# A long convolution and a mode mix by matmul transforms: 45 classes of 128 become 90 classes of 64, with other tiles, buffers and dependency tokens

## The chip, the core and the metric

The kernel runs on one core of one Trainium2 chip. The metric is the time of one execution on the device in microseconds (us); the profile is one execution taken by the hardware profiler. Engines are named as in the profile: PE (matrix engine; PEld is its weight loads), DVE (vector), ACT (scalar), POOL (GpSimd), SP (the engine that issues most DMAs).

## What is computed

```python
B, S, D, n_modes = 8, 5696, 128, 64
def conv(x, h):                       # x [B,S,D], h [S,D]
    L = 2 * S
    Y = rfft(x, n=L, axis=1) * rfft(h, n=L, axis=0)[None]
    return irfft(Y, n=L, axis=1)[:, :S]
def mix(x, w_r, w_i, w_ch):           # w_r, w_i [64,D,D], w_ch [D,D]
    X = rfft(x, axis=1); Y = zeros_like(X)
    Y[:, :64] = complex product of X[:, :64] with w_r + i w_i, per mode
    u = x + irfft(Y, n=S, axis=1)
    return u + maximum(u @ w_ch, 0)
out = mix(conv(x, h), ...)            # float32 [8,5696,128]
```

## The kernel before, in words

The sequence of 5696 is padded to N = 45 x 128. Every transform is a set of matmuls with constant matrices in 16-bit floats, in three steps: over the 45 blocks (constant `F`), then, in each of 45 classes, over the 128 positions in a block (six matrices `M`, real and imaginary parts, each 128 x 5760), then the product with the transformed filter `Hs`, and the way back.

Sequences are taken in pairs (`g_` = 0 to 3). The order of the work is the order in which the Python code adds it, engine by engine:

- **Start.** h is loaded by POOL, the first three `M` by SP, then x of pair 0 by POOL. 16 tiles transform h (128 matmuls of 45 rows), 12 tiles make `Hs`, then 32 tiles `a_tile` (line 338) transform x of pair 0: 8 matmuls of 45 rows each, four per sequence, the two sequences on partitions 0 to 44 and 64 to 108. The evacuation `evac` (line 246) alternates between ACT and DVE. `xtile` gives two PSUM slots of two banks in turn.
- **Ticks.** `tick` (line 365) runs 27 times per pair, two classes a tick. It loads two classes of `Gs` by SP, makes 8 matmuls with `M` (256 columns), ACT copies the result to `Xs`, and DVE makes the complex product by two multiplications (`Pb`, `Xs`) and two half-size additions (`y_part`, line 421). Three ticks later 8 matmuls transform back (`ps<-Xs,M`), ACT or, in one class of eight, DVE copies to `Zs`, and SP writes it to the DRAM scratch `zscr`. Four ticks later 4 matmuls with `Gs` accumulate the 64 low modes in bank 7. Four `Zs` buffers exist. The last four ticks also carry 16 a tiles of the next pair; 16 more follow, and then POOL loads the x after that (`next_x`, line 350). Behind pair 2 it loads the mode weights `W` in eight DMAs instead.
- **Join.** When pair 3 is done, SP loads `IBs`, the `ZT` buffers are cleared in part, 256 matmuls of 8 columns mix the modes, 16 transposes turn them, giving `C`.
- **Output.** `load_zt` (line 496) reads 16 positions of `zscr` back, 45 rows twice, rows 128 KB apart. `u_tile` (line 505) adds the modes' part (360 columns) and the last step over the classes (16 matmuls of 45 columns), 64 tiles in all. `o_tile` (line 525) multiplies four blocks by `[w_ch, I]`, ACT makes `R` (relu), DVE adds (`O`), SP writes 256 KB out. 96 such tiles run, three per two u tiles, and 24 are left at the end. u tiles have two PSUM slots, o tiles two others.

Waits are not written by hand. `Recorder.add` (line 55) derives them from tokens: an operation waits for the last writer of each token that it reads, and for the last writer and all readers of each token that it writes. Tokens need not match memory. In `o_tile` both evacuations write the tokens `HST` of the old filter, whose place their buffers take:

```python
R.add("scalar", lambda e: e.activation(rv, src_r, RELU), bk, [("r", i % NR)] + HST)
R.add("vector", lambda e: e.tensor_tensor(ov, src_u, rv, ADD), bk + [("r", i % NR)], [("o", i % NO)] + HST)
```

Of the kernel before, what the change touches and what calls it, by code (L numbers as in the profile page):

```python
# [4 lines left out]
P = 128  # L5
F16 = mybir.dt.float16
# [117 lines left out]
def bass_long_conv_fft__then__afno_spectral_mix_kernel(nc, x, h, moe_w_r, moe_w_i, moe_w_ch, out):  # L124
# [63 lines left out]
    KW = NQ * P  # L188
    a_m = take(6 * KW * 2)
    m_sb = [at(f"M{i}", KW, F16, a_m + i * KW * 2) for i in range(6)]  # L190
    h_in = at("Hin", P * D, F16, a_m + 3 * KW * 2)
    a_h = take(2 * KW * 2)
    h_sb = at("Hs", 2 * KW, F16, a_h)
    SLOT = 2 * D
    a_as = take(NQ * 2 * SLOT * 2)
    a_sb = at("As", NQ * 2 * SLOT, F16, a_as)
    a_x = take(P * D * 2)
    x_sb = at("Xin", P * D, F16, a_x)
    NG, NX, NB_, NZ = 5, 5, 3, 4
    a_g = take(NG * 1024)  # L200
    g_sb = [at(f"Gs{i}", 512, F16, a_g + i * 1024) for i in range(NG)]
    a_xs = take(NX * 2048)
    x_s = [at(f"Xs{i}", 1024, F16, a_xs + i * 2048) for i in range(NX)]
    a_pb = take(NB_ * 2048)
    p_b = [at(f"Pb{i}", 1024, F16, a_pb + i * 2048) for i in range(NB_)]
    a_zz = take(NZ * 2048)
    z_s = [at(f"Zs{i}", 1024, F16, a_zz + i * 2048) for i in range(NZ)]
    xm = at("XM", B * P, F16, take(2048))
    xt = at("XT", B * P, F16, take(2048))
    xtn = at("XTn", B * 64, F16, take(1024))  # L210
    f1_sb = at("F1", 2 * NQ, F16, take(2 * NQ * 2))
    fq_sb = at("FQ", NQ, F16, take(NQ * 2))
    wi_sb = at("WI", 2 * P, F16, take(512))

    NC = 4
    zt = [at(f"ZT{i}", 4096, F16, a_as + i * 8192) for i in range(NC)]
    ib_sb = at("IBs", KW, F16, a_as + NC * 8192)
    u_sb = [at(f"UT{i}", KW, F16, a_m + i * KW * 2) for i in range(4)]
    NR, NO = 3, 6
    r_sb = [at(f"R{i}", 512, F32, a_h + i * 2048) for i in range(NR)]  # L220
    o_sb = [at(f"O{i}", 512, F32, a_h + (NR + i) * 2048) for i in range(NO)]
    w_sb = at("W", 2 * M * D, F16, a_x)
    yr = at("YR", 512, F16, a_pb)
    yi = at("YI", 512, F16, a_pb + 1024)
    c_sb = at("C", B * P, F16, a_xs)
# [12 lines left out]
    for name, n in (("c", 16), ("x", 12), ("g", 8), ("z", 8), ("w", 16), ("t", 10), ("o", 10)):  # L238
        R.ring(name, n)
# [26 lines left out]


    dma("sync", f1_sb[:, :], c_f1.ap(), "c", (), [("f1",)])
    dma("sync", h_in[NQ - 1:NQ, 64 * D:], c_z.ap(), "c", (), [("hz",)])
    for p0 in (0, 64):  # L270
        dma("sync", x_sb[p0 + NQ - 1:p0 + NQ, 64 * D:], c_z.ap(), "c", (), [("xz", p0)])

    def load_rows(dst, src, off, p0, tok):
        half = 64 * D
        for c in range(2):
            dma("gpsimd", dst[p0:p0 + NQ - 1, c * half:(c + 1) * half],
                bass.AP(src.tensor, src.offset + off + c * half, [[P * D, NQ - 1], [1, half]]),
                "x", (), [tok + (c,)])
# [324 lines left out]
```

## Time and profile before

| what | us |
|---|---|
| three runs | 628.93, 630.63, 630.70 |
| median | 630.63 |
| span of the profiled execution | 636.9 |
| PE busy / PEld busy | 470.4 / 380.9 |
| DVE / ACT / POOL busy | 351.5 / 326.6 / 27.3 |
| share of the last-ending chain: DMA, PE, DVE, ACT | 33%, 28%, 17%, 16% |

The profiled execution's own time is its span, 636.9 us, 6.3 us above the median of the runs. Busy time is an average over the span; the stages differ, so the stretches below are read one by one. [...]

### The profile page before, as it was taken

How to read it: one execution, taken by the hardware profiler on the slowest of the kernel's cores; microseconds unless marked ns; L12 is line 12 of the kernel's file. 1: busy time of each engine (PE TensorE's matmuls, PEld its weight loads, DVE VectorE, ACT ScalarE, POOL GpSimd, SP SyncE). 2: the span in 40 equal slices, each digit the busy share in tenths (PEclk: the TensorE clock that was granted, in tenths of full speed). 3: DMA queues.
4: the chain of work that ended last, by engine and by line, in shares of the span. 5: the costliest groups of instructions: out<-in, count | busy, mean ns of one | idle time of the engine just before them, and what ended most of it. 6: DMA issues, size and time to landing. Idle time of an engine off the chain costs nothing.

```text
span 636.9 us, 11755 instructions
## 1 busy us (share of the span) xinstructions
PE 470.4 (74%) x4924; PEld 380.9 (60%) x4924; DVE 351.5 (55%) x592; ACT 326.6 (51%) x479; POOL 27.3 (4%) x42
## 2 busy tenths in 40 slices
PE   0647769598879598878698868994565877787665
PEld 0647667487667487667487657882543656565432
DVE  0223558398449388448388458883221555555544
ACT  0213547377646476447476547873021555555543
POOL 3000010000010000010000001111200000000000
PEclk9999658799659699559799559998575999999955
DMA  8996119856219856209856209999979999999544
GB/s 155 212 206 252 48 14 144 191 149 179 68 22 139 199 159 169 59 14 148 197 159 169 59 2 147 239 238 244 176 130 181 277 345 346 332 306 341 214 167 167
DMA packets 97546, 110.86 MB, mean 174 GB/s; under 512 B 23147, under 2 KB 81659, under 8 KB 92923
## 3 DMA queue, kind: packets, MB, share of 16 engines
q1 hardware_dynamic: 79398, 92.77, 50.8%
q0 software_dynamic: 18096, 17.35, 19.7%
q8 instruction: 38, 0.62, 0.4%
q14 instruction: 14, 0.11, 0.1%
HBM read 80.53 MB, written 46.92 MB: 200 GB/s over the span
## 4 chain that ended last, share of the span: by engine, by line
DMA 33%; PE 28%; DVE 17%; ACT 16%; issue 5%; SPq 0%; DVEq 0%; ACTq 0%
PE ps L265 28%; DMA zscr<-Zs 8%; DMA M<-cM 7%; DVE O L543 7%; ACT R L542 6%; DMA W<-in_moe_w_i_dram 6%; ACT As L255 5%; DMA W<-in_moe_w_r_dram 5%; DMA out_dram<-O 4%; DMA ZT<-zscr 4%; DVE As L259 4%; ACT Xs L255 2%; DVE Xs L427 2%; DVE Pb L387 2%; DVE Zs L257 1%
## 5 line engine op out<-in xcount | busy, mean ns | idle before, releaser
L265 PE MATMUL ps<-As,M 128*128 128x256 f16 (+1 forms) x900 | 116.2, 283 | 15.8 <-DMA M<-cM 9.5
L259 DVE TENSOR_SCALAR As<-ps 128x720 f16<-128x720 f32 x72 | 67.8, 942 | 94.5 <-PE ps L265 94.5
L265 PE MATMUL ps<-Xs,M 128*128 128x256 f16 x720 | 100.3, 284 | 23.5 <-ACT Zs L253 20.1
L255 ACT ACTIVATE Xs<-ps 128x1024 f16<-128x1024 f32 (+1 forms) x92 | 92.5, 1007 | 46.5 <-PE ps L265 46.2
L255 ACT ACTIVATE As<-ps 128x720 f16<-128x720 f32 x72 | 61.0, 847 | 92.7 <-PE ps L265 92.7
L265 PEld LDWEIGHTS ps<-As,M 128*128 128x128 f16 x900 | 87.8, 107 | 31.6 <-DMA M<-cM 9.7
L253 ACT CAST Zs<-ps 128x512 f16<-128x512 f32 x160 | 88.2, 596 | 35.1 <-DMA zscr<-Zs 26.6
L265 PE MATMUL ps<-F,Xin 45*128 45x90 f16 x1024 | 81.8, 331 | 27.6 <-ACT As L255 15.7
L543 DVE TENSOR_TENSOR O<-ps,R 128x512 f32<-128x512 f32 x96 | 63.1, 658 | 63.5 <-PE ps L265 30.7
L265 PE MATMUL ps<-WI,UT 128*128 128x256 f16 x360 | 70.2, 325 | 35.1 <-DVE O L543 31.5
L265 PEld LDWEIGHTS ps<-F,Xin 45*128 45x128 f16 x1024 | 72.2, 269 | 39.6 <-ACT As L255 21.3
L265 PEld LDWEIGHTS ps<-Xs,M 128*128 128x128 f16 x720 | 71.2, 101 | 37.8 <-ACT Zs L253 20.9
L387 DVE TENSOR_TENSOR Pb<-Xs,Hs 128x1024 f16<-128x1024 f16 (+1 forms) x92 | 62.3, 677 | 56.8 <-ACT Xs L255 56.4
L542 ACT ACTIVATE R<-ps 128x512 f32<-128x512 f32 x96 | 54.9, 572 | 65.4 <-DVE O L543 61.3
L427 DVE TENSOR_TENSOR Xs<-Xs,Pb 128x512 f16<-128x512 f16 (+1 forms) x184 | 77.5, 421 | 0.1
L265 PEld LDWEIGHTS ps<-WI,UT 128*128 128x128 f16 x360 | 42.2, 156 | 56.5 <-DVE O L543 54.6
L265 PE MATMUL ps<-Zs,Gs 128*128 128x256 f16 x360 | 62.7, 290 | 11.5 <-DVE Zs L257 9.8
L391 DVE TENSOR_TENSOR Xs<-Xs,Hs 128x1024 f16<-128x1024 f16 (+1 forms) x92 | 62.0, 674 | 0.1
L265 PEld LDWEIGHTS ps<-FQ,ZT 109*128 109x128 f16 x1024 | 44.3, 101 | 23.3 <-DMA ZT<-zscr 11.2
L265 PE MATMUL ps<-FQ,ZT 109*128 109x45 f16 x1024 | 49.5, 189 | 9.5 <-DMA ZT<-zscr 9.5
L265 PEld LDWEIGHTS ps<-Zs,Gs 128*128 128x128 f16 x360 | 35.3, 104 | 23.3 <-DVE Zs L257 15.3
L265 PE MATMUL ps<-IBs,C 128*128 128x360 f16 x128 | 44.2, 345 | 3.9 <-issue 3.2
(38 smaller groups left out, 199.2 us busy)
## 6 DMA issues: line engine op xcount, KB each, us to landing
ZT<-zscr SPq DMA_DIRECT2D x64, 360.0 KB, 7.5
zscr<-Zs SPq DMA_DIRECT2D x88, 256.0 KB, 3.2
out_dram<-O SPq DMA_DIRECT2D x88, 256.0 KB, 6.1
Xin<-in_x_dram POOLq DMA_DIRECT2D x16, 704.0 KB, 18.3
Gs<-cG SPq DMA_DIRECT2D x88, 128.0 KB, 3.4
M<-cM SPq DMA_DIRECT2D x6, 1440.0 KB, 18.2
W<-in_moe_w_r_dram POOLq DMA_DIRECT2D x4, 512.0 KB, 7.3
W<-in_moe_w_i_dram POOLq DMA_DIRECT2D x4, 512.0 KB, 8.7
```

What stands on the lines that cost most here:

```text
L253: R.add(e, lambda h_: h_.copy(dst, src), reads, writes)
L255: R.add(e, lambda h_: h_.activation(dst, src, COPY, scale=scale), reads, writes)
L257: R.add(e, lambda h_: h_.tensor_copy(dst, src), reads, writes)
L259: R.add(e, lambda h_: h_.tensor_scalar_mul(dst, src, scale), reads, writes)
L265: R.add("tensor", lambda h_: h_.matmul(o, l, r, start=st, stop=sp), reads, writes)
L387: R.add("vector", lambda e: e.tensor_tensor(pbv, xv, hv[1], MULT), [tx] + HST, [tp])
L391: R.add("vector", lambda e: e.tensor_tensor(xv, xv, hv[0], MULT), [tx], [tx])
L427: R.add("vector", lambda e: e.tensor_tensor(a, a, b, ADD if part else SUB), [("xs", s % NX), ("pb", s % NB_)], [("xs", s % NX), ("y", s % ...
L542: R.add("scalar", lambda e: e.activation(rv, src_r, RELU), bk, [("r", i % NR)] + HST)
L543: R.add("vector", lambda e: e.tensor_tensor(ov, src_u, rv, ADD), bk + [("r", i % NR)], [("o", i % NO)] + HST)
```

## The change

The transform length becomes 2S = 11392 = 178 x 64, so that a real transform has 90 classes of 64 positions (89 blocks go in). In parts:

- **First transform:** an a tile has four matmuls of 89 rows, both sequences in one 128-wide weight, 180 columns. Three or four PSUM slots are used outside the ticks, two in the last three ticks, which carry 12 a tiles; 20 follow.
- **Filter:** H's first transform puts real and imaginary part into the two halves of the partitions (weights of 64 columns). The second makes `[hr; hi]` by a matmul of 128 columns of weights, and `[hi; hr]` by two of 64, in each of 90 classes. It now stands behind pair 0's a tiles and behind the issue of pair 1's x.
- **Second transform:** four classes a tick, 16 matmuls of 64 rows and 128 columns, the two sequences in the two halves of the rows. `M` is one 64-row strip, stored twice (4.4 MB instead of 8.8).
- **Product:** two multiplications, `U1` and `U2`, read from ACT's copy in two ticks of three and from PSUM in the third. The additions are left to the third transform, whose two weights `W1`, `W2` are constant: 4 matmuls of 512 columns a tick. ACT makes both copies to `Zs`.
- **Modes:** `G` is loaded once, after H has left its place. Modes lag by three ticks, the third transform by two; a pair has 26 ticks. The turning of the modes moves behind the last pair.
- **Output:** `ZT` has 90 rows, both parts in one DMA of 16 positions, five buffers, no clearing; the twiddles move into the last step's constant `S4` (2.05 MB, loaded behind `IBs`). A u tile covers 8 positions: 16 matmuls of 89 columns and two of 356. u and o tiles share a ring of four PSUM slots; `O` has 12 buffers. `once` puts a token of a reused place only on the first writer.

The core of the diff, cut:

```diff
--- before.py
+++ after.py
@@ -125,50 +125,55 @@
...
+    J = 64
+    NQ = S // J
...
+    KT = 4
+    NT = (NK + KT - 1) // KT
...
+    NU, NXS, NZ = 3, 2, 4
...
+    ZB = 16
+    NC = 5
...
+    next_x(0)
...
+    for i in range(MP):
+        lo, hi = i * KP * 3 * J, (i + 1) * KP * 3 * J + (J if i == MP - 1 else 0)
+        dma("sync", m_sb[:, lo:hi], bass.AP(c_m, lo, [[MW, P], [1, hi - lo]]), "c",
+            HT[:2] if i < 2 else XIN[:2] if i < 4 else [], [("m", i)])
...
+    XSLOT = [0, 2]
+    ZBANK = [4, 5, 6]
     MB = 7
...
     for j in range(16):
-        t = xtile()
+        t = turns("s", [0, 2, 4, 6])
...
+            for ri in range(2):
+                mm(pv(t + i // 4, (i % 4) * NK, [[1, NK]], J * ri, J),
+                   ap(h_in, J * D, 0, NQ, d, [[D, J]]), ap(f1_sb, 2 * NK, 0, NQ, ri, [[2, NK]]),
+                   True, True, HT, [bank(t + i // 4)])
...
+    def a_tile(j, slots):
+        t = turns("s", slots)
+        for i in range(4):
+            d = 4 * j + i
+            mm(pv(t + i // 2, (i % 2) * 2 * NK, [[1, 2 * NK]]),
+               ap(x_sb, 2 * J * D, 0, NQ, d, [[D, 2 * J]]), f1_sb[0:NQ, :], True, True,
+               XIN + [("f1",)], [bank(t + i // 2)])
...
+    for j in range(32):
+        a_tile(j, [0, 2, 4, 6])
+    next_x(1)
...
+    for t in range(NT):
+        n = len(ticks[t])
+        sl = turns("s", [0, 2, 4, 6])
+        for i, k in enumerate(ticks[t]):
+            col = k * 3 * J + J
+            rd = AHT + mtok(k) + [("g", k // KP)]
+            for o, w, c_, p0 in ((0, P, col, 0), (P, J, col + J, 0), (P, J, col, J)):
+                mm(pv(sl + i // 2, (i % 2) * 256 + o, [[1, P]], p0, w), m_sb[:, c_:c_ + w],
+                   ah_sb[:, k * D:(k + 1) * D], True, True, rd, [bank(sl + i // 2)])
+        evac(bass.AP(h_sb, KT * t * D, [[2 * HW, P], [D, n], [HW, 2], [1, D]]),
+             pv(sl, 0, [[256, n], [P, 2], [1, D]]),
+             [bank(sl), bank(sl + 1)], [("h", t)])
+    for i in range(MP):
+        lo, hi = i * KP * P, (i + 1) * KP * P
+        dma("sync", g_sb[:, lo:hi], bass.AP(c_g, lo, [[GW, P], [1, hi - lo]]), "c", (), [("g", i)])
...
+    LC, LM = 2, 3
...
+        i = t % NU
+        hv = [bass.AP(h_sb, r * HW + KT * t * D, [[2 * HW, P], [0, 2], [1, n * D]]) for r in range(2)]
+        uv = [bass.AP(u, 0, [[1024, P], [512, 2], [1, n * D]]) for u in (u1[i], u2[i])]
+        if t % 3 != 2:
+            e = (t - t // 3) % NXS
+            xv = bass.AP(x_s[e], 0, [[1024, P], [512, 2], [1, n * D]])
+            evac(xv, src, bk, [("xs", e)], eng="scalar")
+            src, bk = xv, [("xs", e)]
+        for r in range(2):
+            R.add("vector", lambda e, r=r: e.tensor_tensor(uv[r], src, hv[r], MULT),
+                  bk + [("h", t)], [("u", i, r)])
...
+            for i, k in enumerate(ticks[t]):
+                for r in range(2):
+                    for b in range(2):
+                        col = k * 3 * J + (J if r == 0 else 0) + b * J
+                        mm(pv(sl + b, i * D, [[1, D]]),
+                           ap(m_sb, MW, J * b, J, col, [[1, P]]),
+                           ap(a_sb, AW, J * b, J, (2 * k + r) * D, [[1, D]]), r == 0, r == 1,
+                           AST + mtok(k), [bank(sl + b)])
+            products(t, t)
...
+            s_ = t - LC
+            n = len(ticks[s_])
+            i, zi = s_ % NU, s_ % NZ
+            zb = [turns("z", ZBANK) for b in range(2)]
+            for b in range(2):
+                for r in range(2):
+                    mm(pv(zb[b], 0, [[1, n * D]]), (W1, W2)[r], (u1, u2)[r][i][:, b * 512:b * 512 + n * D],
+                       r == 0, r == 1, [("u", i, r), ("wc",)], [bank(zb[b])])
+                evac(bass.AP(z_s[zi], b * D, [[1024, P], [2 * D, n], [1, D]]),
+                     pv(zb[b], 0, [[D, n], [1, D]]), [bank(zb[b])], [("zs", zi, b)], eng="scalar")
+            zo = (g_ * NK + KT * s_) * P * 256
+            dma("sync", bass.AP(zs, zo, [[256, P], [P * 256, n], [1, 256]]),
+                bass.AP(z_s[zi], 0, [[1024, P], [256, n], [1, 256]]), "z",
+                [("zs", zi, 0), ("zs", zi, 1)], [("zd", g_, s_)])
...
+            s_ = t - LM
+            zi = s_ % NZ
+            for i, k in enumerate(ticks[s_]):
+                mm(pv(MB, 0, [[1, 256]]), g_sb[:, k * P:(k + 1) * P], z_s[zi][:, i * 256:(i + 1) * 256],
+                   k == 0, k == NK - 1, [("g", k // KP), ("zs", zi, 0), ("zs", zi, 1)], [bank(MB)])
...
+            for j in range(12, 32):
+                a_tile(j, [0, 2, 4])
+            if g_ + 2 < NP:
+                next_x(g_ + 2)
+            else:
+                load_w()
...
+    def once(key, toks):
+        if key in first:
+            return []
+        first[key] = 1
+        return list(toks)
+
+    dma("sync", ib_sb[:, :], c_ib.ap(), "c", (), [("ib",)] + once("ib", M_ALL))
+    dma("sync", s4_sb[0:NK, :], c_s4.ap(), "c", (), [("s4",)] + once("s4", M_ALL))
+    zt_old = [AS_ALL, AS_ALL, H_ALL, H_ALL, G_ALL]
+
+    def load_zt(i):
+        g_, c_ = divmod(i, J // ZB)
+        dma("sync", bass.AP(zt[i % NC], 0, [[2 * ZB * 256, NK], [ZB * 256, 2], [1, ZB * 256]]),
+            bass.AP(zs, g_ * NK * P * 256 + c_ * ZB * 256, [[P * 256, NK], [J * 256, 2], [1, ZB * 256]]),
+            "t", [("zd", g_, s_) for s_ in range(NT)], [("zt", i % NC)] + once(("zt", i % NC), zt_old[i % NC]))
+
+    for i in range(NC):
+        load_zt(i)
...
+    LSLOT = [0, 2, 4, 6]
...
+            for pl in range(4):
+                for ri in range(2):
+                    o2 = ri * ZB * 256 + (pl0 + pl) * 256 + b * P
+                    so = ri * S + (c_ * ZB + pl0 + pl) * NQ
+                    mm(pv(t + hb, pl * NQ, [[1, NQ]]), z[0:NK, o2:o2 + P], s4_sb[0:NK, so:so + NQ],
+                       False, pl == 3 and ri == 1, [("zt", i % NC), ("s4",)], [bank(t + hb)])
...
-        R.add("scalar", lambda e: e.activation(rv, src_r, RELU), bk, [("r", i % NR)] + HST)
-        R.add("vector", lambda e: e.tensor_tensor(ov, src_u, rv, ADD), bk + [("r", i % NR)], [("o", i % NO)] + HST)
+        R.add("scalar", lambda e: e.activation(rv, src_r, RELU), bk, [("r", i % NR)] + once(("r", i % NR), G_ALL))
+        R.add("vector", lambda e: e.tensor_tensor(ov, src_u, rv, ADD), bk + [("r", i % NR)],
+              [("o", i % NO)] + once(("o", i % NO), AS_ALL if i % NO < 6 else H_ALL))
...
+            for half in range(2):
+                u_tile(i, b, half)
+                nt += 1
+                for _ in range(2 if nt % 2 == 0 else 1):
+                    if todo:
+                        o_tile(*todo.pop(0))
+        if i + NC < NB:
...
```

## Rows read from the trace of the kernel before

**Rows 1.** Stretches: length, busy of PE, PEld, DVE, ACT, POOL (count); clock, DMA share, GB/s.
```profile
65.60:93.60 28.00, 20.56 (x256) 18.18 (x256) 13.82 (x17) 14.17 (x16) 0.00 (x0) 0.57 0.01 4
157.00:187.70 30.70, 23.83 (x282) 20.22 (x282) 15.99 (x18) 15.59 (x20) 0.00 (x0) 0.63 0.17 48
439.00:467.50 28.50, 11.61 (x318) 10.50 (x319) 5.67 (x6) 2.07 (x5) 4.28 (x4) 0.55 0.88 182
467.50:492.70 25.20, 14.93 (x252) 10.61 (x249) 4.54 (x5) 7.26 (x10) 0.00 (x0) 0.70 0.93 170
492.70:601.70 109.00, 83.31 (x1142) 65.29 (x1142) 62.38 (x91) 61.66 (x103) 0.00 (x0) 0.97 0.94 313
```

**Rows 2.** Timeline, pair 1: start, length, engine, line, names, count, idle before.
```profile
224.74 0.39 PE L265 MATMUL ps<-Zs,Gs 128*128 128x256 f16 x2 [0.44 <-DVE Zs L257]
...
227.15 1.04 PE L265 MATMUL ps<-As,M 128*128 128x256 f16 x8
...
229.14 1.07 ACT L253 CAST Zs<-ps 128x512 f16<-128x512 f32 x2
...
229.33 1.04 PE L265 MATMUL ps<-As,M 128*128 128x256 f16 x8
...
234.09 0.39 PE L265 MATMUL ps<-Zs,Gs 128*128 128x256 f16 x2 [0.44 <-DVE Zs L257]
```

**Rows 3.** Chain of waits in order of time: start, length, what.
```profile
197.00 16.49 DMA zscr<-Zs
...
380.01 6.38 DMA W<-in_moe_w_r_dram
...
437.98 9.90 DMA W<-in_moe_w_i_dram
```

**Rows 4.** Timeline, the last o tiles, ACT and DVE.
```profile
619.01 0.60 ACT L542 ACTIVATE R<-ps 128x512 f32<-128x512 f32 x1 [0.87 <-DVE O L543]
619.70 0.69 DVE L543 TENSOR_TENSOR O<-ps,R 128x512 f32<-128x512 f32 x1 [0.78 <-ACT R L542]
...
620.49 0.60 ACT L542 ACTIVATE R<-ps 128x512 f32<-128x512 f32 x1 [0.87 <-DVE O L543]
```

**Rows 5.** Page, part 2: GB/s moved in 40 slices of 15.9 us.
```profile
GB/s 155 212 206 252 48 14 144 191 149 179 68 22 139 199 159 169 59 14 148 197 159 169 59 2 147 239 238 244 176 130 181 277 345 346 332 306 341 214 167 167
```

**Rows 6.** Timeline, PE, first transforms of h and of x.
```profile
21.37 17.77 PE L265 MATMUL ps<-F,Hin 45*128 45x90 f16 x128 [21.37 <-DMA Hin<-in_h_dram]
...
83.42 1.28 PE L265 MATMUL ps<-F,Xin 45*128 45x90 f16 x16 [0.48 <-ACT As L255]
```

**Rows 7.** Timeline, PE, matmuls of 128 and of 45 columns.
```profile
57.78 1.96 PE L265 MATMUL ps<-As,M 128*128 128x128 f16 x32 [0.43 <-DVE Hs L259]
...
562.39 0.36 PE L265 MATMUL ps<-FQ,ZT 109*128 109x45 f16 x8
```

**Rows 8.** Timeline, PE, where 128 x 128 meets another shape.
```profile
161.16 0.60 PE L265 MATMUL ps<-Zs,Gs 128*128 128x256 f16 x4
161.69 1.23 PE L265 MATMUL ps<-F,Xin 45*128 45x90 f16 x16
...
563.49 0.30 PE L265 MATMUL ps<-WI,UT 128*64 128x256 f16 x1 [0.38 <-DVE O L543]
563.72 0.33 PE L265 MATMUL ps<-IBs,C 128*128 128x360 f16 x1
```

**Rows 9.** Groups by line and shape: count, busy us, mean ns, idle before.
```profile
L255 ACT ACTIVATE Xs<-ps 128x1024 f16<-128x1024 f32 x88 | 90.0, 1025 | 46.5 <-PE ps L265 46.2
L387 DVE TENSOR_TENSOR Pb<-Xs,Hs 128x1024 f16<-128x1024 f16 x88 | 60.6, 689 | 56.8 <-ACT Xs L255 56.4
L259 DVE TENSOR_SCALAR Hs<-ps 128x1024 f16<-128x1024 f32 x5 | 6.1, 1225 | 18.7 <-PE ps L265 18.7
```

**Rows 10.** Issues of DMAs, as in the page's part 6: KB each, median us to landing.
```profile
ZT<-zscr SPq DMA_DIRECT2D x64, 360.0 KB, 7.5
...
IBs<-cIB SPq DMA_DIRECT2D x1, 1440.0 KB, 6.5
```

More of the change, by code (lines that the diff above doesn't have):

```diff
@@ L186, in take @@
         return off
[L188 to L201, printed above, removed]
@@ L213, in bass_long_conv_fft__then__afno_spectral_mix_kernel @@
[L213 to L221, printed above, removed]
+    AW, HW, GW = NK * 2 * D, NK * D, NK * P
+    a_as = take(AW * 2)
+    a_sb = at("As", AW, F16, a_as)
@@ new lines, in bass_long_conv_fft__then__afno_spectral_mix_kernel @@
+    a_x = take(2 * J * D * 2)
+    x_sb = at("Xin", 2 * J * D, F16, a_x)
+    a_m = take(MW * 2)
+    m_sb = at("M", MW, F16, a_m)
+    a_h = take(2 * HW * 2)
+    h_sb = at("Hs", 2 * HW, F16, a_h)
+    a_g = take(GW * 2)
+    g_sb = at("G", GW, F16, a_g)
+    ah_sb = at("Ah", HW, F16, a_g)
+    NU, NXS, NZ = 3, 2, 4
+    a_st = take((2 * NU + NXS + NZ) * 2048)
+    h_in = at("Hin", J * D, F16, a_st)
+    u1 = [at(f"U1_{i}", 1024, F16, a_st + i * 4096) for i in range(NU)]
+    u2 = [at(f"U2_{i}", 1024, F16, a_st + i * 4096 + 2048) for i in range(NU)]
@@ new lines, in bass_long_conv_fft__then__afno_spectral_mix_kernel @@
+    x_s = [at(f"Xs{i}", 1024, F16, a_st + NU * 4096 + i * 2048) for i in range(NXS)]
+    z_s = [at(f"Zs{i}", 1024, F16, a_st + NU * 4096 + (NXS + i) * 2048) for i in range(NZ)]
+    a_xm = take(2048)
+    xm = at("XM", B * P, F16, a_xm)
+    xtn = at("XTn", B * M, F16, take(1024))
+    f1_sb = at("F1", 2 * NK, F16, take(2 * NK * 2))
+    wc_sb = at("Wc", 4 * P, F16, take(4 * P * 2))
+    xt = at("XT", B * P, F16, a_st)
+    ZB = 16
+    NC = 5
+    zt_off = [a_as, a_as + 16384, a_h, a_h + 16384, a_g]
@@ new lines, in turns, with load_rows @@
+    def turns(name, items):
+        i = ring2.get(name, 0)
+        ring2[name] = i + 1
+        return items[i % len(items)]
+    QA = 80
+    dma("sync", f1_sb[0:NQ, :], c_f1.ap(), "c", (), [("f1",)])
+    def load_rows(dst, src, off, col, tok):
+        for q0, n in ((0, QA), (QA, NQ - QA)):
+            dma("gpsimd", bass.AP(dst, q0 * dst.shape[1] + col, [[dst.shape[1], n], [1, J * D]]),
+                bass.AP(src.tensor, src.offset + off + q0 * J * D, [[J * D, n], [1, J * D]]),
+                "x", (), [tok + (q0,)])
@@ new lines, in bass_long_conv_fft__then__afno_spectral_mix_kernel @@
+    AS_ALL = AST
+    H_ALL = [("h", t) for t in range(NT)]
+    U_ALL = [("u", i, r) for i in range(NU) for r in range(2)] + [("xs", i) for i in range(NXS)] + \
+            [("zs", i, b) for i in range(NZ) for b in range(2)]
+    M_ALL = [("m", i) for i in range(MP)]
+    G_ALL = [("g", i) for i in range(MP)]
+    first = {}
+    def once(key, toks):
[4 more added lines that the diff above has]
+    dma("sync", ib_sb[:, :], c_ib.ap(), "c", (), [("ib",)] + once("ib", M_ALL))
@@ L523, in bass_long_conv_fft__then__afno_spectral_mix_kernel, with o_tile @@
+        src = pv(t, 0, [[1, NQ], [512, 2], [NQ, 4]])
+        evac(bass.AP(u_sb[ub], c_ * ZB + half * 8, [[S, P], [J, NQ], [4, 2], [1, 4]]),
+             src, [bank(t), bank(t + 1)], [("u_", ub, 2 * c_ + half)] + once(("u", ub), old), eng=e)
     n_o = [0]
-    def o_tile(g_, b, r4, slot):
+    NW = S // P
+    TAIL = S - NW * P
+    def o_tile(g_, b, r4):
         ub = (g_ % 2) * 2 + b
         bb = 2 * g_ + b
-        t = 4 + 2 * slot
+        t = turns("l", LSLOT)
         i = n_o[0]
         n_o[0] += 1
-        full = r4 < 11
+        full = r4 < NW // 4
```

380 lines of the change are left out of this document (125 added, 255 removed).

## The prediction, made before any run of the changed kernel

> **What bounds the kernel now.** I read the stretches first, because the average over the span (PE 74%, DVE 55%, ACT 51%) mixes stages with different limits [rows 1]. The span falls into four parts: the start up to the first sequence pair's ticks (to 93.6 us), four pairs of some 95 us each, a join from 439 to 492.7 us that waits for transfers, and the output part up to 636.9 us.
>
> Inside a pair, a steady tick is bound by PE. The groups of `As,M` matmuls start 2.18 us apart without a pause, and 20 matmuls of 256 columns at (1.04 - 0.27)/7 = 0.11 us are 2.18 us. On every fourth tick PE waits for the one `Zs` copy that DVE makes, so four ticks take 234.09 - 224.74 = 9.35 us, 2.34 each [rows 2]. The chain of waits then shows a stall that no engine causes: a `zscr` write takes 16.5 us because the next pair's x load occupies the DMA engines. It stands in the chain three times, once in each of the first three pairs. In the last pair eight W loads run from 380.0 to 447.9 us [rows 3].
>
> [...]
>
> In the output part the reader should look at who waits for whom. ACT's `R` starts only when DVE's previous `O` has ended, and `O` only when its `R` has: 620.49 - 619.01 = 1.48 us per o tile, with PE, its banks and the buffers all free [rows 4]. The code says why: every `R` and every `O` writes the same tokens (`HST`, lines 542 and 543), so the recorder chains them all. 96 o tiles x 1.475 = 142 us, which is the stretch from 492.7 us to the end. Up to 601.7 us the DMA engines are 94% busy there at 313 GB/s [rows 1].
>
> **Part by part.** Times are of the profiled execution, whose span of 636.9 us is 6.3 us above the 630.63 us median; I take that off at the end.
>
> Start. h, x and M share the DMA engines at about 200 GB/s (the first three slices) [rows 5]. Counted as the queues count them, h is 1.46 MB, two sequences 2.9 MB, M now 4.4 MB instead of 8.8. The M loads now wait on SP for h, and later for x; only more M pieces and small constants queue behind them, and nobody needs those yet. So h lands near 11 us and both sequences near 37 us (8.8 MB / 200 GB/s = 44 us for all, with a quarter of the bytes of M still to come). H's first transform runs inside that time. Then 32 a tiles. Each now has 4 weight loads with a strided source instead of 8. One after the other such pairs of load and matmul take 17.77/128 = 0.139 us; in the a tiles of before, where two 45-row matmuls lie in different halves of the array, 16 take 1.28 us, so two go at once [rows 6]. With 89 rows there is no second half: 4 x 0.14 = 0.56 us. Evacuation is 0.89 us on either engine for every second tile, 0.45 per tile [rows 1], and three or four slots instead of two take the latency away. I take 0.58: 19 us, to 56.
>
> [...]
>
> H's second transform mixes a 128-column matmul with two of 64 columns in every class. The rows price a change of the array's shape: four matmuls of 256 columns start at 161.16 and the first of the other shape at 161.69, so 0.53 instead of 0.44 us; a 64-column one at 563.49 delays the next full one by 0.23 us where its columns are 0.11 [rows 8]. I take 0.2 us from start to start at each change: 90 classes x (0.2 + 0.02 + 0.2) = 38 us at the high clock, and up to 49 if the clock is granted at half, as in the a tiles. Take 44: ticks start at 100 us, not at 94.65. Without those changes it would be 90 x 3 x 0.057 (1.96 us for 32, the last one's tail taken off) = 15 us [rows 7].
>
> [...]
>
> The moved x load of pair 1 now runs behind H's second transform, and pair 0 loses its stall (16 us). G (2.95 MB) stands on SP ahead of pair 0's z writes, but each piece goes as soon as H has left its place.
>
> Ticks. PE: 16 half-height matmuls of 128 columns, in pairs on the two halves: 7 x 0.057 + 0.2, then 4 x 0.216 of 512 columns, then 3 x 0.109 + 0.2 for the modes: 2.0 us. ACT: 1.02 in two ticks of three, plus two copies (1.07 together), 1.75 on average [rows 2, 9]. DVE: two products at 0.69, in every third tick from PSUM, which I bound by 0.69 below and by the 1.23 us of a 1024-element PSUM read above: at most 1.74 [rows 9]. The two additions of a tick go into the third transform's accumulation. I take 2.1 us. The pairing is seen on 45 rows with strided weights only, so its bounds here are both ways: one at a time would make the tick 2.45. 21 full ticks and 2 short ones: about 47.5 us.
>
> Between pairs: 12 a tiles in the last ticks at the old 0.9 (two slots), 20 at 0.58: 23 us, where before has 30.7. Pair 0 so takes 70.5 us. Pairs 1 and 2 keep the x stall: the first z write returns 26 us in, then 17 ticks x 2.1 + 23 = 85 us each (96.6 before). Pair 3 has 53 us of ticks. End of ticks: 100 + 70.5 + 85 + 85 + 53 = 393 us, against 439.
>
> Join. W starts when pair 3's a tiles end, near 340, and needs 62 to 68 us as before: 402 to 408, and 14 us of mode mixing follow. Beside it SP sends IB (6.5 us) [rows 10], S4, which by the shared tokens waits for IB to land, and five ZT buffers, of which the second and fourth wait for the one before. The resident G and the missing memsets save nothing here.
>
> Output. The false chain is gone: `once` gives the shared tokens to a buffer's first use alone. An o tile then costs DVE 0.69 and ACT 0.60 [rows 4], PE 4 x 0.11. A u tile costs PE more: at 0.11 us per 256 columns, 16 matmuls of 89 and two of 356 are 16 x 0.04 + 2 x 0.15 = 0.94 us, against 0.70 with 45 columns at 0.025. Three o and two u tiles: PE 3.2, ACT and DVE 2.75 us, against 4.42 before. So transfers become the bound. ZT alone ran at 170 GB/s with the engines 93% busy, and beside the output at 2 x 369 kB in 4.42 us, 167 GB/s [rows 1, 10]; I take 180 GB/s as its limit. S4 and ZT are 25.7 MB: 143 us, plus 6.5 for IB, 4 of bubbles. After the last ZT come 4 u and 30 o tiles: 24 us, and 3 for the last write. That is 393 + 180 = 573 if ZT is the limit throughout; by the sum of all transfers (49 MB at 345 GB/s, the best slices) [rows 5] it is 393 + 156 = 549. The two are equally near to the rows; I take the middle, 560 us, or **553 us** by the median.
>
> **Rivals.** (1) The half-height matmuls go one after the other: 78 ticks x 0.45 = +35, 588 us. For it: dense 128-column weights on 64 rows appear nowhere. Against it: two at once in [rows 6]. (2) ZT isn't limited, because its reads lie differently in DRAM now: the output part is bound by PE, 24 x 3.3 + 17 from about 435: 530 us, less with a short H. For it: beside the output the o tiles set the pace, so no row shows that ZT could not have gone faster there. (3) Slower: the same new spacing makes the ZT reads slower. The point is where S4 and ZT take 206 us, 125 GB/s; at 110 GB/s the span is 664, the time 658 us. Against it: 170 GB/s [rows 1], with rows twice as far apart. (4) The chain of o tiles stays in another form: 447 + 142 + 3 = 592 of span, 585 us. The tokens speak against it.
>
> **How the numbers follow.** Forecast 0.53, rival 1 0.13, rival 2 0.20, rival 3 0.05, rival 4 0.05, others 0.04. The range 518 to 597 us takes in rivals 1, 4 and most of 2, and the bounds of H (11 us), of a tick (0.1 us each way) and of the two output sums. A measurement of this kernel can tell about 0.3% from no change. Slower by more than that needs rival 3 or a second surprise: 0.06. Within 0.3%: 0.01. Faster: 0.93.
>
> **What would show it.** H's second transform at 38 to 49 us with PE mostly idle; ticks 2.0 to 2.2 us apart, with half-height matmuls two at a time; no zscr stall in pair 0, one in pairs 1 and 2; `O` no longer following each `R` in lockstep, and PE or ACT waiting for ZT instead. The prediction is wrong if PE waits for nothing in the output part (rival 2), or if o tiles still come 1.48 us apart (rival 4).

## The result and the profile after

The changed kernel takes **563.37 us** (median of 4 runs, 558.86 to 564.82) where the kernel before took 629.78 beside it: a ratio of 0.89, 95% interval 0.8833 to 0.8966. The forecast was 553 us, 518 to 597. The profiled execution has a span of 561.1 us (before 636.9); the prediction's sum for it was 560. Its two parts, up to the end of the ticks and from there on, were wrong by some 25 us each, in opposite directions, and most of what follows is about them. A run that took over 1.5% longer than the fastest of its kernel is left out of the comparisons below.

The stretches of the changed kernel, columns as in [rows 1]: H's first transform, pair 0's a tiles, H's second transform, the four pairs, and the output part. The DMA share adds up the time of all packets, so it can pass 1, as it does in pair 3. The clock is the share of its full speed that PE was granted.

```profile
12.30:32.40 20.10, 19.09 (x257) 18.96 (x257) 7.26 (x8) 6.16 (x8) 0.00 (x0) 1.00 0.99 205
32.40:51.60 19.20, 19.20 (x128) 19.20 (x129) 13.60 (x15) 13.19 (x16) 0.00 (x0) 1.00 0.37 148
51.60:93.60 42.00, 42.00 (x272) 20.84 (x270) 13.92 (x12) 11.67 (x12) 2.04 (x4) 1.00 0.58 129
93.60:163.40 69.80, 65.63 (x672) 45.84 (x671) 51.55 (x64) 53.15 (x79) 0.79 (x2) 0.90 0.31 93
163.40:240.60 77.20, 69.21 (x670) 46.84 (x670) 52.06 (x62) 52.41 (x79) 1.77 (x5) 0.81 0.46 115
240.60:319.20 78.60, 67.92 (x670) 46.52 (x670) 51.25 (x63) 52.26 (x78) 2.23 (x4) 0.83 0.46 114
319.20:368.20 49.00, 46.42 (x542) 26.50 (x543) 35.85 (x46) 37.88 (x62) 9.03 (x9) 0.96 1.37 200
368.20:394.00 25.80, 9.62 (x285) 8.65 (x284) 1.12 (x2) 3.46 (x11) 0.00 (x0) 0.55 0.81 210
394.00:428.90 34.90, 22.66 (x305) 18.86 (x305) 5.40 (x6) 7.52 (x10) 0.00 (x0) 0.75 0.82 192
...
460.00:500.00 40.00, 32.93 (x426) 28.11 (x424) 22.00 (x34) 21.79 (x38) 0.00 (x0) 0.91 0.99 320
```

The ticks end at 368.2 us where they ended at 439: 71 us earlier. The output part takes 561.1 - 368.2 = 192.9 us where it took 197.9 [rows 1]. So nearly the whole gain was made before the output part, although the change removes the chain of o tiles there. Two rows point at why the output part gave so little: PE has 9.62 us of work in the first 25.8 and 22.66 in the next 34.9, and the DMA engines, 82% busy, move only 192 GB/s. In these two stretches PE waits for ZT, as the prediction said; from the first o tiles on it hardly does, and DVE waits for output writes instead. Over the span (page, part 5, last columns: idle before, and what ended it), then from 428.9 us on (engine, waited for: us, times, longest):

```profile
L276 PE MATMUL ps<-S,ZT 90*128 90x89 f16 x1024 | 71.0, 221 | 25.0 <-DMA ZT<-zscr 24.9
```

```profile
DVE O L565 <- DMA out_dram<-O: 27.6, 8, 10.8
...
PE ps L276 <- DVE O L565: 23.3, 10, 10.3
...
PEld ps L276 <- DMA ZT<-zscr: 1.0, 2, 0.7
```

In the ticks (timeline of PE in pair 0: start, length, names, count) one tick of four classes is now

```profile
120.20 0.62 PE L276 MATMUL ps<-As,M 64*128 64x128 f16 x16
120.75 1.04 PE L276 MATMUL ps<-U,Wc 128*128 128x512 f16 x4
121.63 0.60 PE L276 MATMUL ps<-Zs,G 128*128 128x256 f16 x4
122.16 0.62 PE L276 MATMUL ps<-As,M 64*128 64x128 f16 x16
```

122.16 - 120.20 = 1.96 us. Sixteen half-height matmuls start and end within 0.62 us; one after the other, at the 0.057 us that one of 128 columns takes [rows 7], they would take 0.91. So two run at once. Rival 1 (no pairing, 2.45 us a tick) is out.

The chain of waits in order of time (start, length, what):

```profile
169.05 12.87 DMA zscr<-Zs
...
245.84 13.89 DMA zscr<-Zs
...
328.89 7.17 DMA zscr<-Zs
...
337.24 7.93 DMA zscr<-Zs
...
368.38 6.36 DMA IBs<-cIB
...
375.15 18.70 DMA ZT<-zscr
...
394.74 15.58 DMA ZT<-zscr
...
412.92 29.03 DMA ZT<-zscr
441.95 22.73 DMA out_dram<-O
```

Pair 0 has no stalled z write in this chain, pairs 1 and 2 have one each; in the last pair, where the chain of the kernel before had W [rows 3], three z writes of 7 to 8 us stand beside the W loads. From 368 to 442 us the chain is transfers but for 2.6 us of PE: IB, then S4 with the first ZT, then later ZT transfers. Three more waits for output writes, 17 to 19 us each, follow up to 521 us.

### The profile page after: what moved, and what is told of

Same layout as the page of the kernel before. It is cut to its first block, busy times and chain, and to the rows that moved or that the text cites. A ratio compares the mean times of both kernels' runs of the same rounds, so it can differ in the third digit from the quotient of the medians.

```text
span 561.1 us, 11554 instructions
## 1 busy us (share of the span) xinstructions
PE 463.3 (83%) x4998; PEld 337.1 (60%) x4998; DVE 305.4 (54%) x391; ACT 310.5 (55%) x481; POOL 19.3 (3%) x31
## 4 chain that ended last, share of the span: by engine, by line
PE 51%; DMA 37%; ACT 5%; DVE 4%; issue 1%; SPq 0%; DVEq 0%; POOL 0%; ACTq 0%; POOLq 0%
PE ps L276 51%; DMA out_dram<-O 14%; DMA ZT<-zscr 11%; DMA zscr<-Zs 9%; ACT Zs L264 2%; DMA Hin<-in_h_dram 2%; DVE As L270 2%; DVE U L396 2%; ACT As L266 1%; DMA IBs<-cIB 1%; ACT R L564 1%; ACT Xs L264 1%; DVE O L565 1%; SPq L273 0%; ACT UT L264 0%
## 5 line engine op out<-in xcount | busy, mean ns | idle before, releaser
L264 ACT CAST Zs<-ps 128x512 f16<-128x512 f32 (+1 forms) x184 | 100.2, 603 | 36.5 <-DMA zscr<-Zs 19.5
L276 PE MATMUL ps<-U,Wc 128*128 128x512 f16 (+1 forms) x368 | 98.6, 390 | 12.3 <-ACT Zs L264 12.3
L396 DVE TENSOR_TENSOR U<-Xs,Hs 128x1024 f16<-128x1024 f16 (+1 forms) x128 | 80.3, 671 | 51.5 <-ACT Xs L264 50.4
L276 PE MATMUL ps<-S,ZT 90*128 90x89 f16 x1024 | 71.0, 221 | 25.0 <-DMA ZT<-zscr 24.9
L565 DVE TENSOR_TENSOR O<-ps,R 128x512 f32<-128x512 f32 x96 | 59.2, 652 | 53.2 <-DMA out_dram<-O 27.6
L276 PE MATMUL ps<-F,Xin 89*128 89x180 f16 x512 | 80.9, 345 | 8.5 <-DVE As L270 4.4
L276 PEld LDWEIGHTS ps<-S,ZT 90*128 90x128 f16 x1024 | 63.5, 109 | 36.4 <-DMA ZT<-zscr 26.8
L276 PEld LDWEIGHTS ps<-F,Xin 89*128 89x128 f16 x512 | 75.4, 224 | 13.6 <-DVE As L270 6.0
L264 ACT CAST Xs<-ps 128x1024 f16<-128x1024 f32 x64 | 63.1, 993 | 14.0 <-PE ps L276 14.0
L276 PE MATMUL ps<-As,M 64*128 64x128 f16 x1440 | 61.7, 232 | 5.5 <-DVE As L270 2.2
L396 DVE TENSOR_TENSOR U<-ps,Hs 128x1024 f16<-128x1024 f32 x56 | 65.8, 1217 | 0.3 <-PE ps L276 0.2
L276 PEld LDWEIGHTS ps<-Zs,G 128*128 128x128 f16 x360 | 35.0, 99 | 24.3 <-ACT Zs L264 3.8
## 6 DMA issues: line engine op xcount, KB each, us to landing
out_dram<-O SPq DMA_DIRECT2D x88, 256.0 KB, 12.5
```

The source lines that it names most:

```text
L264: R.add(e, lambda h_: h_.copy(dst, src), reads, writes)
L276: R.add("tensor", lambda h_: h_.matmul(o, l, r, start=st, stop=sp), reads, writes)
L396: R.add("vector", lambda e, r=r: e.tensor_tensor(uv[r], src, hv[r], MULT), bk + [("h", t)], [("u", i, r)])
```

## The experiments

In the edits, lines are cut to the part that changes, and `...` stands for lines left out.

**1. What H's second transform pays.** The 128-column matmul of each class is split, so that all four of a class have one shape. The same sums come out.

```diff
-            for o, w, c_, p0 in ((0, P, col, 0), (P, J, col + J, 0), (P, J, col, J)):
+            for o, w, c_, p0 in ((0, J, col, 0), (0, J, col + J, J), (P, J, col + J, 0), (P, J, col, J)):
```

> The changed kernel, with H's second transform made of 64-column matmuls alone (four in a class instead of one of 128 and two of 64): the same sums, no change of the array's shape. In the changed kernel the stage takes 41.8 us, 0.464 a class. [...] The x load of pair 1 (issued where the stage starts, 25 us) then ends at about pair 0's first z write, so little of it stalls: time 541 to 548 us. Rival B (a class is bound by the evacuation or the weights, not the shape): stage 40 us or more, time 560 to 566.

Measured: 541.21 us (538.95 to 542.73), ratio to before 0.8601 (0.8538 to 0.8663), 22 us under the changed kernel. The stage shrinks from 42.0 to 17.7 us, at a granted clock of 1.00 in both. The groups of this stage by shape (count, busy, mean ns), the changed kernel first:

```profile
L276 PE MATMUL ps<-Ah,M 128*64 128x128 f16 x180 | 28.5, 315 | 0.0
L276 PE MATMUL ps<-Ah,M 128*128 128x128 f16 x90 | 25.9, 288 | 0.0
```

and the experiment:

```profile
L276 PE MATMUL ps<-Ah,M 128*64 128x128 f16 x360 | 12.8, 227 | 5.2 <-issue 4.9
```

A third more matmuls, and PE is busy 12.8 us where it was busy for all 42.0. The stage lost 24.3 us and PE 29.2, which over 180 changes of shape are 0.135 and 0.16 us each. The two differ because PE waits in the shorter stage, where DVE's copies to `Hs` stand in the chain. Rival B is out. The change of shape is what this stage pays, 42.0 us with it and 17.7 without, and the expected 541 to 548 us, which rest on that, hold. Of the edits here that keep the output, this one gained most.

**2 and 3. What the chain of o tiles is worth.** In the changed kernel the chain is put back (one shared token written by each `R` and each `O`); in the kernel before it is taken out (`HST` at a buffer's first use alone).

```diff
-bk, [("r", i % NR)] + once(("r", i % NR), G_ALL))
+bk, [("r", i % NR), ("line",)] + once(("r", i % NR), G_ALL))
...
-              [("o", i % NO)] + once(
+              [("o", i % NO), ("line",)] + once(
```

> The changed kernel with one token added that every R and every O writes, as HST did before: nothing else. Theory A (transfers bind the output part now; the chain of 1.475 us per o tile is about as slow as they are while ZT is read, and slower only for the last 24 o tiles): 96 x 1.475 = 142 us from the first o tile at 429 us, end at 574 to 580 of span, time 576 to 582 us, 13 to 19 more. Rival B (the chain was what held the output part, and its removal is worth what was forecast): 33 us or more, time over 596. Rival C (transfers bind everywhere, the chain costs nothing): within 3 us of 563.

Measured: 584.04 us (583.89 to 585.32), ratio 0.9291 (0.9216 to 0.9367), 21 us above the changed kernel: just over theory A's range, and well under rival B's. The waits of the output part (engine, waited for: us, times, longest) show the lockstep again:

```profile
ACT R L564 <- DVE O L565: 68.3, 87, 7.5
DVE O L565 <- ACT R L564: 39.4, 54, 0.9
```

In the kernel before:

```diff
-bk, [("r", i % NR)] + HST)
+bk, [("r", i % NR)] + (HST if i < NR else []))
...
-[("o", i % NO)] + HST)
+[("o", i % NO)] + (HST if i < NO else []))
```

> The kernel before, with the tokens HST only on the first use of each R and O buffer; nothing else. Theory A (transfers at 313 GB/s and 94% busy engines bound the stretch to 601.7 us beside the chain): that stretch shortens by at most 10%, and the 24 last o tiles, bound by two PSUM slots and the writes, come at 0.75 to 1.1 instead of 1.475 us: 10 to 25 us gained, time 605 to 620. Rival B (the chain alone bound it): three o and two u tiles fall from 4.42 to about 3 us, 35 us or more gained, time under 595. Rival C: no gain, 627 to 632.

Measured: 617.14 us (614.84 to 620.76), ratio 0.9816 (0.9734 to 0.9898): some 12 us less than the kernel before measured beside it (629.44 us), where the o tiles' pace alone, 96 x (1.475 - 0.69) [rows 4], would have given 75. That is theory A's range. The stretch that answers to the last of [rows 1]:

```profile
492.00:600.00 108.00, 81.72 (x1103) 64.94 (x1101) 66.28 (x99) 65.37 (x110) 0.00 (x0) 0.95 0.91 327
```

327 GB/s against 313 [rows 1], at nearly the same busy share of the engines (0.91 against 0.94). The chain was real, but what comes next is nearly as slow: from 480 us on, waits for output writes are 39% of the chain of waits of this run. Transfers are the likely limit under the chain; no run here tests that in the kernel before.

**4 and 5. Two suspected causes that were not it.** First, the classes' rows in DRAM further apart (66.5 instead of 64 KB); then the ZT transfers on POOL's queue, so that no output write stands behind them in one queue.

```diff
+    ZR = P + 5
-    zs = nc.dram_tensor("zscr", [NP * NK * P, 2 * D], F16, kind="Internal")
+    zs = nc.dram_tensor("zscr", [NP * NK * ZR, 2 * D], F16, kind="Internal")
...
```

The z writes and the ZT reads use `ZR` in place of `P` in the same way.

> The changed kernel with 2560 bytes of space behind each class in the DRAM scratch, so that the rows that a ZT transfer reads lie 66.5 KB apart instead of 64 KB; the same bytes and descriptors. Theory A (the spacing in DRAM makes the ZT reads slow): ZT alone goes faster than the 188 GB/s of 375 to 410 us (250 or more), and the output part shrinks by 15 to 40 us, time 525 to 548. Rival B (the DMA engines or the destination set the rate): 180 to 195 GB/s again, time 559 to 567.

Measured: 563.26 us (559.56 to 566.22); the first ZT takes 18.74 us (18.70). The power-of-two spacing is not the cause.

```diff
-        dma("sync", bass.AP(zt[i % NC], 0,
+        dma("gpsimd", bass.AP(zt[i % NC], 0,
```

> The changed kernel with the 16 ZT transfers issued by POOL instead of SP, so that a write of the output no longer stands behind 1.47 MB of ZT in one queue. In the changed kernel DVE waits 27.6 us for output writes, which land 12.5 us after their issue. Theory A (order in the queue costs the output part): writes land in under 8 us, these waits go to under 8 us, time 545 to 556. Rival B (the engines' total work binds, whoever goes first): time 558 to 568, and PE waits for ZT in place of DVE for the writes.

Measured: 561.24 us (560.22 to 563.51), ratio 0.8922 (0.8861 to 0.8982). The time is rival B's, but neither picture came out. Over the span the writes land in 4.1 us (median) instead of 12.5; while ZT runs, from 428 to 500 us, in 19.1 instead of 15.9. From 428 us on DVE waits 33.3 us for them instead of 27.6. So the order in one queue is not what makes the writes late, and the transfers at work beside them remain.

**6 and 7. ZT and writes apart.** One kernel issues the first five ZT transfers only, the other only the short writes of the last 64 rows.

```diff
-        if i + NC < NB:
+        if False:
             load_zt(i + NC)
```

> The changed kernel without the last 11 ZT transfers: the u tiles from the sixth on work on what the first five brought, so the numbers that come out are others. It shows what the output part takes when the writes and the engines bind it. Theory A (transfers bound it): from the first o tile at 429 us the end comes in 24 x 3.3 + 17 = 96 us, less the waits in the first pair, span 515 to 530. [...]

Measured in a single run: 532.03 us, with a span of 530.2 us, at the upper end of theory A. DVE waits for no output write from 428 us on, and the writes land in 2.8 us (median).

```diff
+        if not full:
             dma("sync", dst, src, "o", [("o", i % NO)])
```

> The changed kernel without the 256 KB output writes (only the eight tails of 64 rows are written; the rest of the output is left out). ZT runs alone. Theory A (ZT has a limit of its own near 190 GB/s): the 16 transfers still come some 7.8 us apart, the last u tile at 515 to 522 us instead of 539.8, span 535 to 545. Rival B (only the sum of all transfers binds): ZT speeds up to 300 GB/s, last u tile before 490, span under 515.

Measured in a single run: 544.98 us, with a span of 543.2 us, in theory A's range; the last u tile comes at 524.7, a little after it. The stretch in which ZT has the DMA engines almost to itself:

```profile
428.00:500.00 72.00, 63.34 (x824) 54.12 (x823) 41.49 (x63) 41.20 (x71) 0.00 (x0) 0.90 0.95 224
```

The engines are 95% busy at 224 GB/s. So ZT has a limit of its own that no other transfer causes. Without the later ZT transfers 31 us are gone, without the writes 18.

**8 and 9. What the limit hangs on.** ZT is written to 90 rows of SBUF. Here the transfers of the first three pairs carry 128 rows (42% more bytes, the surplus unused), then 96.

```diff
+        nr = P if g_ + 1 < NP else NK
-        dma("sync", bass.AP(zt[i % NC], 0, [[2 * ZB * 256, NK], [ZB * 256, 2], [1, ZB * 256]]),
-            bass.AP(zs, g_ * NK * P * 256 + c_ * ZB * 256, [[P * 256, NK], [J * 256, 2], [1, ZB * 256]]),
-            "t", [("zd", g_, s_) for s_ in range(NT)],
+        dma("sync", bass.AP(zt[i % NC], 0, [[2 * ZB * 256, nr], [ZB * 256, 2], [1, ZB * 256]]),
+            bass.AP(zs, g_ * NK * P * 256 + c_ * ZB * 256, [[P * 256, nr], [J * 256, 2], [1, ZB * 256]]),
+            "t", [("zd", q_, s_) for q_ in range(g_, min(g_ + 2, NP)) for s_ in range(NT)],
```

The second edit has 96 in place of the first `P`.

> The changed kernel with ZT transfers of 128 rows instead of 90 for the first three pairs: 38 rows of the next pair's classes are read along and never used, 42% more bytes. Transfers of 128 rows ran fast here (IB: 1.46 MB in 6.4 us, 230 GB/s with its latency; ZT of 90 rows: 188). Theory A (the rate hangs on which rows of SBUF the engines write at a time): a transfer of 2.1 MB takes no longer than the 7.8 us of 1.47 MB, 270 GB/s or more, the first pair's u tiles end no later, time 555 to 572. Rival B (DRAM or the count of bytes sets the rate): 11 us a transfer, some 30 us more in all, time over 585.

Measured: 547.98 us (545.94 to 549.38), ratio 0.8714 (0.8659 to 0.8769): 15 us faster with more to carry, beyond what theory A gave. The stretch between the first ZT and the first o tile, and the issues of ZT (KB each, median us to landing):

```profile
396.00:427.00 31.00, 24.03 (x320) 20.35 (x318) 6.39 (x8) 8.12 (x11) 0.00 (x0) 0.76 0.89 358
```

```profile
ZT<-zscr SPq DMA_DIRECT2D x12, 2048.0 KB, 16.7
```

358 GB/s at a busy share of 0.89, against 192 at 0.82 in the changed kernel's stretch from 394.0, where a ZT of 1440 KB lands after 19.0 us (median over the span). An 8 KB packet takes 0.33 us on average there, against 0.56 (averages over the packet records of those stretches).

> The changed kernel, but the ZT transfers of the first three pairs carry 96 rows instead of 90 (the rows from 90 on are the first classes of the next pair and go unused). In the trace of the changed kernel 90 rows keep 15 DMA engines busy and an 8 KB packet takes 0.56 us; with 128 rows it was 16 engines and 0.33 us. 96 rows spread over 16 engines too, six to each. Theory A: what counts is that all of SBUF's rows are written at once, so that the engines don't meet at the same part of it; 96 rows leave the packets at 0.50 to 0.57 us and the time at 555 to 570 us. Theory B: what counts is that all 16 engines take part evenly; then 96 rows bring the packets down to 0.31 to 0.36 us, and with a quarter less to carry than 128 rows the time is 536 to 548 us.

Measured: 563.03 us (561.17 to 566.52), ratio 0.8968 (0.8883 to 0.9052): no gain.

```profile
394.00:431.00 37.00, 22.07 (x308) 18.41 (x309) 5.45 (x7) 7.52 (x10) 0.00 (x0) 0.79 0.85 196
```

```profile
ZT<-zscr SPq DMA_DIRECT2D x12, 1536.0 KB, 18.8
```

96 rows keep 16 packets in flight for most of the time and 90 rows 15, by the packet records, but a packet takes 0.57 and 0.56 us. So it isn't the number of engines at work, and theory A is what is left of the two: fast, at 0.33 us a packet, are here the transfers whose 128 rows cover SBUF. That cause is argued, not shown, since no transfer of 90 rows placed otherwise in SBUF was tried. One more pair of transfers in the changed kernel fits it. By the packet records IB (128 rows, 1.46 MB) takes 4.8 us, 302 GB/s, and S4 (90 rows, 2.05 MB) 11.8 us, 174 GB/s; both are constants with each row in one piece, so the slow rate belongs neither to the scratch `zscr` nor to 8 KB packets.

The 192 and 196 GB/s in these stretches, and the 224 for 90 rows where the engines are 95% busy (experiment 7), are about half of the 424 that transfers of 128 rows reach in experiment 11.

**10 and 11. Both edits together, and a free start.** The kernel with edits 1 and 8, and the same with the first transfers of the output part no longer chained by shared tokens: each waits for the part of `M`, `As` or `Hs` that it overwrites.

> The changed kernel with two of the edits above together: H's second transform in matmuls of one shape, and ZT transfers of 128 rows. Theory A: the two lie in different stages and add: 563.4 - 22.2 - 15.4 = 526 us, 522 to 530. Theory B: the shorter H stage pushes the x load of the second pair into the first pair's ticks, where it costs a part again: 531 to 540 us.

Measured: 527.60 us (525.03 to 528.23), ratio 0.8386 (0.8334 to 0.8439). The two gains add (theory A). Its chain after the ticks:

```profile
346.47 6.52 DMA IBs<-cIB
...
353.39 18.19 DMA ZT<-zscr
...
372.17 13.12 DMA ZT<-zscr
385.31 8.77 DMA ZT<-zscr
```

```diff
-once("ib", M_ALL)
+once("ib", M_ALL[3:])
-once("s4", M_ALL)
+once("s4", M_ALL[:3])
-    zt_old = [AS_ALL, AS_ALL, H_ALL, H_ALL, G_ALL]
+    zt_old = [AS_ALL[:16], AS_ALL[16:], H_ALL[:16], H_ALL[16:], G_ALL]
```

> As the kernel with both edits, and the first transfers of the output part no longer wait for each other: IB, S4 and the first four ZT buffers overwrite different parts of M, As and Hs, and each now waits only for the tokens of its own part. In the run with ZT of 128 rows alone, first u tile 398 and first o tile 426 us, 30 and 58 us after the ticks end, with IB 6.5, S4 and ZT 17.0, ZT 13.4 and ZT 8.9 us one after the other in the chain; the mode mixing is done at 384. Theory A: that start is what the serial transfers cost; 11.9 MB at some 350 GB/s are 34 us, so the first o tile comes 12 to 20 us earlier and so does the end: 506 to 515 us. Theory B: later on the ZT transfers and the writes together set the pace, and what the start gains is waited for there: 518 to 528 us.

Measured: **516.21 us** (512.20 to 517.43), ratio 0.8197 (0.8144 to 0.8249). The chain and the stretches that follow:

```profile
350.28 37.80 DMA ZT<-zscr
```

```profile
369.00:390.00 21.00, 19.27 (x309) 16.47 (x307) 6.26 (x7) 7.92 (x11) 0.00 (x0) 0.87 1.01 424
390.00:430.00 40.00, 34.07 (x447) 29.48 (x445) 23.22 (x36) 23.27 (x42) 0.00 (x0) 0.91 1.02 419
```

One wait of 37.8 us in place of 46.6 in four pieces. The first o tile starts 44 us after the ticks end instead of 56, and the end comes 11.4 us earlier. The time lies 1 us above theory A's range and below theory B's: the start's gain is kept, with no sign that a later limit takes it back. This is the fastest version of the study, 47 us under the changed kernel.

**12. What a running x load costs the ticks.** The loads of x for the last two pairs are left out.

```diff
-            if g_ + 2 < NP:
-                next_x(g_ + 2)
-            else:
+            if g_ + 2 == NP:
                 load_w()
```

> The changed kernel without the x loads of the third and fourth pairs (these pairs compute on the second pair's x, so the output is not the reference's). What a running x load costs a pair's ticks is in dispute: the prediction gave pairs 1 and 2 85 us each, with a first z write that returns 26 us into the pair; the changed kernel took 77.2 and 78.6, with 18.5 and 19.1 us. Theory A: the stalled z write is the whole difference to the first pair, which takes 69.8 us without one; pairs 1 and 2 (beside which the loads of x for the third and fourth pairs ran) shrink to 69 to 71 us each and the time is 545 to 550 us. Theory B: the later pairs are slower for another reason (the lower granted clock there, 0.81 and 0.83 against 0.90, or the DVE and ACT order), and at most half of the 16 us comes back: 555 to 560 us.

Measured in a single run: 546.75 us, span 545.0. The pairs' ticks start at 93.7, 163.6, 233.7 and 304.9 us, so pairs 1 and 2 take 70.1 and 71.2 us instead of 77.2 and 78.6, and the chain has no stalled z write in them. The granted clock is 0.84 in both, hardly above the 0.81 and 0.83 with the loads, so theory B's clock is not the reason. Theory A: the x load, through the z write that it stalls, is the difference. In the last pair two stalls stay in the chain, beside W:

```profile
314.50 7.08 DMA zscr<-Zs
...
322.77 7.95 DMA zscr<-Zs
```

## Why the prediction was right, and where it was not

The direction and the size hold: 563.4 us lies 10 above the forecast of 553. Of these, 1 is the span, 561.1 against the sum of 560. The other 9 come from the last step: the prediction took off 6.3 us, by which the span of the profiled execution before lay above the median, and here the span lies 2.3 us below it. That the sum for the span came out within 1 us is luck, as the steps show. Step by step, in the profiled execution:

**Start.** h has landed at 12.3 us (forecast 11), and the a tiles start at 32.4, not 37. They take 19.2 us for 32, 0.60 each (0.58). H's second transform takes 42.0 us (44). The profile counts PE as busy throughout, so the sign "PE mostly idle" did not show, but experiment 1 shows that the changes of shape are what it pays: its 17.7 us stand against the 15 foretold without changes. Ticks start at 93.6, not 100. PE is busy for all of the 19.2 us of the a tiles, 0.150 us for each of 128 matmuls (0.139 in [rows 6]), and 0.60 us a tile stands above the evacuation's 0.45. Before, 32 of them took 28.0 us at a granted clock of 0.57 [rows 1], 0.875 each, which is the prediction's old 0.9.

**Ticks.** 1.96 us against 2.1, just under the 2.0 to 2.2 foretold. Pair 0 takes 69.8 us (70.5). Pairs 1 and 2 were mis-sized: 77.2 and 78.6 us against 85. The working was 26 us until the first z write returns, and 59 after. The 59 hold, 240.6 - 181.9 = 58.7. The 26, copied from before [rows 3], were too many: the write returns 18.5 us into pair 1. Beside the x load the engines are as busy as before and move more (the kernel before, then the changed one, columns as in [rows 1]):

```profile
187.70:213.50 25.80, 17.34 (x134) 13.50 (x132) 15.73 (x32) 12.84 (x18) 3.00 (x6) 0.83 0.94 149
```

```profile
163.40:182.00 18.60, 14.12 (x166) 8.36 (x166) 10.91 (x14) 9.16 (x14) 1.24 (x3) 0.78 0.98 198
```

The G stream, which ran there before, is gone, and the load's rows lie differently; which of the two it is was not tried. Experiment 12 shows that without the x loads these pairs take 70.1 and 71.2 us, as pair 0 does. Pair 3 takes 49.0 us (53) in spite of its stalls behind W. All in all the ticks end 25 us before the forecast: 6 from the start, 1 from pair 0, 14 from pairs 1 and 2, and 4 from pair 3. The join did not bind: the mode mixing was done at 382 us, where the prediction had 416 to 422.

**Output part.** Forecast 167 us as the middle of two sums, 156 by all bytes and 180 by ZT's limit; measured 192.9. (The 0.025 us for 45 columns comes from the kernel before, where eight such matmuls take 0.36 us [rows 7] and five 0.29. 49 MB at 345 GB/s are 142 us; 156 comes out with the 6.5, 4 and 3 us of the other sum, which the prediction doesn't say.) The sum by ZT's limit was nearly exact in its main term. By the packet records the last ZT lands at 519.3 us, 151 us after the ticks end, where 143 for S4 and ZT, 6.5 for IB and 4 for bubbles make 153.5. Experiments 7 and 8 show that ZT has a limit of its own. That this limit is 180 GB/s is in part luck: alone ZT moves 224, and without the writes its last transfer lands 17 us earlier, at 502 us (experiment 7). So the first failing step is the choice of the middle, 13 us: "the two are equally near to the rows" was not so, since ZT stood in the rows at 170 GB/s, alone [rows 1], and no row had shown it faster. The second is the tail. The prediction left 4 u and 30 o tiles after the last ZT, 24 us and 3 for the write. There were 11 u and 42 o tiles, and 561.1 - 519.3 = 41.8 us: 15 too few. It counted tiles as if those that had their data were done. But by the code the last of the 16 ZT transfers goes out when 20 u tiles are still to come, since its buffer must be free, and it lands 17.9 us later. At the prediction's own 3.2 us for two u and three o tiles, at most 11 u tiles are done by then, which leaves 9. The output writes are not needed for this lag: experiment 7, without them, has 14 u and 46 o tiles and 41 us behind its last ZT.

The waits for writes shown above, 27.6 us of DVE and 23.3 of PE, hold the tiles up, for the most part ahead of the last ZT. The writes share the DMA engines with ZT and land late, a median of 12.5 us over the span against 3.8 in its last 61 us, when ZT ends, so the `O` buffers run out, DVE waits, and PE waits for its banks. In experiment 6, without the later ZT transfers, DVE waits for no write there. The issues of writes (KB each, median us to landing), over the span and then from 500 us on:

```profile
out_dram<-O SPq DMA_DIRECT2D x88, 256.0 KB, 12.5
...
out_dram<-O SPq DMA_DIRECT2D x51, 256.0 KB, 3.8
```

The two errors, 25 us too slow ahead of the output part and 26 too fast in it, cancelled to 1 us of span. They have nothing to do with each other, so this is luck.

**Rivals.** Rival 2 (ZT not limited) falls by experiments 6 and 7. Rival 3 (a slower ZT because of the spacing in DRAM) needs 125 GB/s or less; ZT alone moved 192 to 224, and experiment 4 clears the spacing. Rival 4 (a chain that stays) gave 585 us; experiment 2, which puts it back, gave 584.0. The agreement is luck: the o tiles started at 431 us, not 447, and took 148 us, not 142. The chain was worth 21 us in the changed kernel and some 12 in the one before, far less than the o tiles' pace alone would give, because transfers set nearly the same pace.

## What to carry to other kernels

A lockstep in the timeline shows that a chain exists, not what it is worth: look for the transfer or engine that would set the pace next, and price the difference to that. Where a row shows a transfer slow while it runs alone, take that rate as its limit until a row shows it faster, and count the work behind its last byte from the moment its last buffer comes free, not from what has its data. A token shared by several buffers orders everything that writes it: splitting those tokens between the buffers was worth 11 us.

## What the runs showed of the hardware

- The ZT transfers from DRAM to SBUF move 358 to 424 GB/s here with 128 rows, 192 to 224 with 90 (engines 82 and 95% busy) and 196 with 96 (85%). Padding them with 42% of unused bytes made the kernel 15 us faster (experiments 7, 8, 9 and 11).
- Matmuls with weights of 64 and of 128 columns in turn cost 0.135 us of the stage for each change, 0.16 of PE (experiment 1).
- A load on POOL's queue that keeps the DMA engines busy holds up 256 KB writes from SP: 12.9 and 13.9 us beside x and 7 to 8 beside W, against a median of 2.3 over all of them in the same kernel.
